# A complex power table on VectorE: rows of 80 bytes, second products in a tile of their own, exponents in another order, and a new order of all steps

## The chip, the cores and the metric

The kernel runs on one core of a Trainium2 chip. A core has five engines that run side by side and meet through semaphores: TensorE (PE in the profile; its weight loads are PEld), VectorE (DVE), ScalarE (ACT), GpSimd (POOL) and SyncE (SP), which here issues the DMAs. The metric is the device time of one execution in microseconds (us); a time of the kernel is the median of several runs.

## The reference

Two branches on the same input `x` (2048 tokens x 512), mixed by a gate per token:

```python
g = sigmoid((x * gate_w).sum(-1, keepdims=True))
a = A(x)      # attention in 4 segments of 512 tokens, 32 heads of 16, with a running memory
b = B(x)      # state-space convolution over all 2048 tokens, per channel
return g * a + (1 - g) * b
```

Branch B builds a kernel of 2048 lags for each of the 512 channels from 128 complex states, and convolves by FFT:

```python
logdA = dt * (A_re + 1j * A_im)
l = arange(2048).astype(bf16)
P = exp(logdA[:, :, None] * l)                 # 512 x 128 x 2048 powers
K = einsum('dn,dnl,dn->dl', Cc, P, dt * Bc).real
y = irfft(rfft(pad(x)) * rfft(pad(K)))[:, :2048] + x * Dskip
```

Since `l` is rounded to bf16, only 640 different lags occur. Each is a sum of one of 20 exponents and one of 32 exponents, so the powers are products of two small tables.

## The kernel before

**Branch A.** For each of 4 segments and 4 groups of 8 heads, PE projects q, k and v and makes the scores in five parts (`scores`, tags A0, B0, C, A1, B1). ACT takes each part's exponential, 128x2048 at a time (L1128, 80 in all); DVE applies the causal mask to half of them (L1140). PE multiplies by v, DVE normalises (L1100 to L1103). The result goes through a DMA transpose or PE into the tile oT.

**Branch B, tables.** `ssm_powers` squares z = exp(dt A) nine times, so that `pws[(k, h)]` holds z to the power 2^k for half h of the channels. `tables(c)` runs four times, once for each 128 channels. It fills two tables in SBUF, with 4 bytes (two states in bf16) for each entry:
- table F has 20 slots, one for each exponent of `F_EXP`, and 4 spare slots behind them: a row of 24 slots is 96 bytes, and there are 128 rows, 64 in each of two planes (real and imaginary);
- table G has 32 slots, for multiples of 8, and 8 spare ones: rows of 160 bytes.

Four slots of F and one of G are copied in (L1253, L1256; engine chosen by the order). The others come from `cmul` (L1226): it multiplies n slots at `src`, `src + sstep`, ... by z^(2^k) and writes them to the n slots from `dst`. A complex product is two real products and a sum. With sources that are neighbours (`sstep == 1`), one DVE instruction makes both products (L1236), the second going to the spare slots `sp`. Otherwise there are two instructions, one for each product (L1241). Then a sum (L1245) adds the spare slots, planes exchanged, to the destination. F has six such steps, G also six. Then 128 small matmuls a table (`64x40`, tags lag) multiply G by F, and the lag values go through `kex` and four DMAs to the tile KTT.

**Branch B, convolution.** `conv` has 32 steps u. A spectrum of x comes from `x_level1` through DRAM (Zx) and a matmul (X). The constants CD come by DMA into one of 4 buffers. PE makes the spectrum of K from CD and KTT, a cast takes it to SBUF, DVE multiplies (L1371, tags Y), PE transforms back (tags V), a cast takes V to SBUF, and a DMA puts its rows into the tile V2. Steps 0 to 15 fill V2[0], steps 16 to 31 fill V2[1].

**The end.** `finals` makes 16 results of 128x512. Each is a sum in PSUM of matmuls over oT and `wo` (tags fin, fih) and over V2 (fir reads V2[0], fis V2[1]). Results 0 to 7 are taken out in two parts and pass a float32 tile (L1405 prepares it, L1427 adds, L1441 writes out), results 8 to 15 in one scaled copy (L232 on ACT or L233 on DVE).

**The order.** Nothing is scheduled while the kernel is built. The string `ORDER` lists every operation by its number, in the order in which each engine runs it; `a` or `v` behind a number says whether a copy that either engine could make runs on ACT or DVE (`evac`: L229 and L232 on ACT, L230 and L233 on DVE), and the numbers behind a slash choose the buffers. `replay` reads it and `emit` puts the semaphore waits in. DMAs are operations of SP in the same list, issued in their order: one that waits holds up those behind it.

Of the kernel before, what the change touches and what calls it, by code (L numbers as in the profile page):

```python
# [8 lines left out]
BF16 = mybir.dt.bfloat16  # L9
# [365 lines left out]
15/0 16/0 9/0 37/4/0 38 0/0 10/1 31/0/0 32a 7/0 47/0 13/2 1203/0 29/5 30a 17/1 40/1 18 19 39/2 46/3 42/4 20 49/5 43 44  # L375
45 21 48/6 50 41/7 53/0 65/1 55/8 51 52 1214/6/0 5/0 66/2 12/3 54/9 58/0 68/7 56/10 1209/3/1 60/11 1/0 57 72/1 59/12
63/0 61/13 73v/0 62 11/4 3/0 70/0 71 64 1215v 69v/0 82/1 83/2 84 27/0 202/0 33/0/1 34a 218/0 203 67v 23/0 4/0 96/3
26/0 14/5 94/2 95 85v/1 76/3 1211/1 206/0 1212a 1216/0 213/2/0/0 209/4 106/0 77/4 214a 86 1210a 263/1/1/1 264a 97v/2
204 35/2/2 268/5/0/0 189/5 210/0 108/6 36a 74 24/0 223/3 22/0 107 118/1 78 390/0 109v/3 120/7 215 184/0 227/1/1/1
820/0 1213 119 88/2 89/1 224a 269 270 605/0 187/3 98 130/0 1217a 110 131/2 1206/2/1 133a/4 132 185/1 121a/5 122  # L380
407/3/1 228 1204/0 216/6/0 217a 134 144/3 253/0/0 254 111 408a 142/2 1224/1 2/0 230 123 1205a 255 90 190/0 1207a 186/0
188 192/1 1019a/0 145v/6 143 219/3 75 220v 606/0 146 157v/7 232/0/1 1023 271 233 154/3 155/7 1024 135 607 821/2 100/2
229 234 99 1027 1218 822 156 1028 158 221/3 1029 1018v/0 211/0 1030 1221/0/0 205/0 222a 1219/1 1017a 147 1220a 1208
1245/0 265 159 168/6 1031 241/0/2 242 212/0 1222a 243 1032 306/2/2/2 307a 1015a 225/3 226a 236/0/3 237 1223 235/1 238
266/0/1 308 1230/2/1 267a 1231a 1038 87 1016a 239 240 169v/8 279/0/1 166/3 167 28/0 1020 102/0 1225/3/0 1226a 1227/0
244 245/1 1228a 1232/2 280 1229 281 1237/3/0 1021 1039 350/0/2 351a 249/0/3 250 246 1022 170 1233a 1234 231/0/0 272
247/0 347/2/3/0 251 248/1 284/0/2 1238a 285 1040 178v/9 348a 391/3 392 171 273/0 252 286 1263/2/1 1264a 256 1025
1235/3 1236a 257 258/2 393 275/0/3 276 277 1026 1261/0 179 180 1041 311/2/1/1 312 352/3/0/0 259 1239 353 1033 101
112/3 260 1034 313 1035 296/0/0 297 298 354 309/1/0 314 278/2 1262a 1242/3/0 310a 1265 292/0/3 293 355 1036 113/5 282
283 315/0 1037 1243a 1042 356 291/1 114 1043 294 124/2 349 287 1240/3 1241a 1044 1045 288/3 1046 357 333/0/1 334 335  # L390
1051/3/0 1052 395/1 1053 126/2 125 136/3 1055/0 1056 1057a 193 191 1054a 207 320/0/2 137/3 138 321 1047/0 322 289 1048
1049 1050a 1061/0 150/7 295 208 1066v/0 299 300 1064v/0 1063v 1248/3/1 1070 1062v 301/4 1065a 1067 1071 302 1266/1
316/0/3 317 1249a 318 1068 290/1 1246/0 1247a 1060 1059 396/3/0/1 397a 1069 148/2 1074 337/0/0 338 319/2 323 139v/3
1072 149 1073 303 1080 409/0 339 1075 140 1076 410a 160/1 1077 325/0/3 103a/0 104 324 1244 1250 326 505/3/1/2 141 1081
327 1078 398 1082 457/1/1 458a 506a 359/0/2 360 361 332/0 336 91a/1 340 328 161/6 341 342/5 1083 115v/5 304 1084 105
1253/1/0 1254a 1251/3 1252a 1255 329/0 343 1089 363/0/1 364 330 1269/1/1 79v/2 365 399/3/0 1079 127a/8 400a 1090
368/0/3 369 1270a 116 370 117 1272/3/0 411/1 92 412a 80 1273a 162 81 93 172/0 331/1 376/0/0 377 362/2 366 367 371
405/1 1091 378 163v/4 406a 1274/3 344 128 1058 345 413/0/1/1 129 414 380/0/2 1085 175v/6 1275a 1086 1092 381 382 375/1
379 261 415 1267/3 1268a 164 454/0/2/0 455a 165 418/0/1 419 420 1271 1087 176 177 1093 456 383 1088 384 385/1 624/3/0
461/0 625a 462/0/0/0 463 174/2 403/1 464 422/0/3 423 465 1098/3/0 372/2 424 1099 386 1276 1094/0 1095 1096 1097a 404  # L400
1100 1101a 435/0/0 416 387/1 373 151v/9 374 173 181v/7 1291/0 436 437 1102/1 1103 1277/0/1 274 1258/2/0 1259a 1256/3
439/0/2 1257a 1112v/0 1278a 440 1322/1 1113v/0 441 1111a 152 557/2/2 1104v 1106 558a 153 1117 182 421/1 1279/3 1118
507 1260 388 1121 427/0/1 428 1284/0/0 1110v 1122 1109v 1280a 425 1105 426 183 1282/2 1123 1114 429 1285a 1124 262/0
417/3/1 466 478/0/3 1283a 479 434/0 1115 1281 1125 1116 438 442 1126 6/0 1119 608 480 430 1107 431/3 1120 1309/2 443
444/4 1127 626/2 432 467 1128 401/0 627a 1286 1108 473/0/0 474 475 8/0 305 445 669/2/3/1 459/1 402 469/0/1 433/0 470
670a 1129 513/3/1/1 471 1301/0 194/1 446 508/2/0 509a 1132 1130 195/0 486/0/2 487 514 515 488 1310/0/0 1131 460 472/2
476 1287/0 1302/1/0 1303a 1288/1 1289/3/1 477 1290a 1311a 1136 1133 1137 1134 481 490/0/1 1138 491 492 485/1 489 1135
554/3/0/0 555a 1314/2 1292/0/1 1139 1140 1304/3 1293a 346 535/0/0 536 537 556 614/3/1 1370/4 615a 1305/0/2 1306a 394/0
493 494 495/0 1307/4 610/0 824 496 482/5 562/5/0/0 1294/6 563 565 1145/3/0 564 358 1141/0 1308a 1146 1295a 1147 1148a
1340/1 483 484/1 516 1142 1143 1144a 539/0/3 540 497 541 498/1/1/0 1317/2 1149/0 1150 1151a 1327/0 199/0 196 671 512/0  # L410
# [98 lines left out]
F_EXP = [1, 3, 6, 8, 2, 4, 262, 264, 258, 260, 5, 7, 520, 516, 776, 772, 1032, 1288, 1544, 1800]  # L509
# [1023 lines left out]
```

## Time and profile before

| | us |
|---|---|
| median of 3 runs | 300.8 (299.62 to 302.68) |
| the profiled execution, its own time | 297.4 |
| its span, first to last instruction | 295.6 |
| PE busy | 256.1 |
| DVE busy, 609 instructions | 270.6 |
| ACT busy, 326 instructions | 262.1 |
| mean granted TensorE clock | 0.971 |

The profile is of one execution. A row of its groups has the line, the engine, the operation, what is written and read with shapes, the number of instructions, their busy time together, the mean length of one in ns, and the idle time of the engine just before them with what ended it. An instruction's length reaches from its start to its result; on DVE and ACT the next one can start a little before that. The line of a copy is that of the helper `evac`.

### The profile page before, as it was taken

What the parts mean: (1) busy time and instruction counts of PE and PEld (TensorE: products, weight loads), DVE (VectorE), ACT (ScalarE), POOL (GpSimd) and SP (SyncE); (2) the same over time, 40 slices, a digit from 0 to 9 for tenths busy, and PEclk for the clock granted to TensorE, in tenths of its full rate; (3) what the DMA queues carried; (4) which work ended last, traced back from release to release, by engine and by line L of the source; (5) the groups of instructions that cost most, each with busy time, mean ns of one, the idle gap of its engine ahead of it and who ended that gap; (6) DMA issues with size and microseconds to landing.
All of it is one profiled execution on the core that took longest, in us unless ns stands there. A gap on an engine that the chain in (4) does not pass through costs nothing.

```text
span 295.6 us, 8579 instructions
## 1 busy us (share of the span) xinstructions
PE 256.1 (87%) x3517; PEld 151.7 (51%) x3563; DVE 270.6 (92%) x609; ACT 262.1 (89%) x326; POOL 3.2 (1%) x9
## 2 busy tenths in 40 slices
PE   5786887789878797899998899999998999999992
PEld 2343344464445563576663655555554454547661
DVE  2989999989999999999999999999899999987792
ACT  5989999989999999999999999999999999985120
POOL 2000000000000000000000000000000000000000
PEclk9979799957999999999999999999999999999999
DMA  5999712105224358226754368767676867994124
GB/s 127 259 259 202 219 39 86 42 2 159 55 54 124 115 157 202 84 65 164 178 104 118 81 190 233 199 178 200 185 220 162 221 196 177 243 215 120 38 109 174
DMA packets 60600, 44.00 MB, mean 149 GB/s; under 512 B 34577, under 2 KB 55954, under 8 KB 60562
## 3 DMA queue, kind: packets, MB, share of 16 engines
q1 hardware_dynamic: 60562, 43.46, 55.7%
q8 instruction: 28, 0.46, 0.7%
q14 instruction: 10, 0.08, 0.1%
HBM read 22.08 MB, written 7.86 MB: 101 GB/s over the span
## 4 chain that ended last, share of the span: by engine, by line
DVE 48%; PE 26%; ACT 18%; issue 5%; DMA 1%; SPq 0%; DVEq 0%
PE psum L704 25%; DVE sb L1236 13%; ACT sb L1128 10%; DVE sb L1245 9%; ACT sb L229 6%; DVE sb L1241 4%; DVE sb L230 3%; DVE sb L1103 1%; DVE sb L1140 1%; DVE sb L850 1%; DVE sb L849 1%; DVE sb L1182 1%; DVE sb L1009 1%; DVE sb L1371 1%; DVE sb L857 1%
## 5 line engine op out<-in xcount | busy, mean ns | idle before, releaser
L704 PE MATMUL psum<-sb 128*128 128x17 bf16 (+13 forms) x3429 | 250.9, 238 | 32.8 <-ACT sb L1128 12.9
L704 PEld LDWEIGHTS psum<-sb 128*128 128x128 bf16 (+5 forms) x3475 | 145.6, 101 | 133.2 <-ACT sb L1128 33.6
L1128 ACT ACTIVATE sb<-psum 128x2048 bf16<-128x2048 f32 x80 | 151.6, 1895 | 4.6 <-PE psum L704 3.8
L229 ACT ACTIVATE sb<-psum 128x512 bf16<-128x512 f32 (+4 forms) x162 | 88.3, 595 | 10.4 <-PE psum L704 8.3
L1236 DVE TENSOR_TENSOR sb<-sb 128x1024 bf16<-128x1024 bf16 (+3 forms) x36 | 48.8, 1358 | 0.1
L230 DVE CAST sb<-psum 128x512 bf16<-128x512 f32 (+3 forms) x51 | 31.0, 619 | 3.1 <-PE psum L704 2.9
L1245 DVE TENSOR_TENSOR sb<-sb 128x512 bf16<-128x512 bf16 (+3 forms) x48 | 33.4, 700 | 0.1
L1140 DVE TENSOR_TENSOR sb<-sb 128x1024 bf16<-128x1024 bf16 (+1 forms) x40 | 22.7, 579 | 1.1 <-ACT sb L1128 0.9
L1371 DVE TENSOR_TENSOR sb<-sb 128x1024 bf16<-128x1024 bf16 x32 | 21.8, 681 | 0.9 <-ACT sb L229 0.4
L1241 DVE TENSOR_TENSOR sb<-sb 128x512 bf16<-128x512 bf16 (+1 forms) x24 | 15.2, 632 | 0.5 <-ACT sb L229 0.3
L1103 DVE TENSOR_TENSOR sb<-psum,sb 128x256 bf16<-128x256 f32 x32 | 13.5, 421 | 0.4
L232 ACT ACTIVATE sb<-psum,sb 128x512 bf16<-128x512 f32 x5 | 3.4, 687 | 11.5 <-PE psum L704 11.5
L848 ACT ACTIVATE sb<-sb 128x512 f32<-128x512 f32 x18 | 11.4, 656 | 0.3 <-DVE sb L849 0.3
L1427 DVE SCALAR_TENSOR_TENSOR sb<-psum,sb 128x512 f32<-128x512 f32 x8 | 5.9, 748 | 2.9 <-PE psum L704 2.9
L1182 DVE TENSOR_TENSOR sb<-psum,sb 128x512 bf16<-128x512 f32 x12 | 8.3, 689 | 0.3
L849 DVE TENSOR_TENSOR sb<-sb 128x256 f32<-128x256 f32 x18 | 7.6, 420 | 1.1 <-ACT sb L848 1.0
L1100 DVE RECIPROCAL sb<-psum 128x16 f32<-128x16 f32 x32 | 8.0, 251 | 0.4 <-PE psum L704 0.3
L1059 ACT ACTIVATE sb<-sb 128x512 bf16<-128x512 bf16 x12 | 7.6, 633 | 0.1
L850 DVE SCALAR_TENSOR_TENSOR sb<-sb 128x256 f32<-128x256 f32 x18 | 7.6, 420 | 0.0
L1008 ACT ACTIVATE sb<-psum 128x512 bf16<-128x512 bf16 x12 | 7.3, 623 | 0.0
L857 DVE CAST sb<-sb 128x512 bf16<-128x512 f32 x15 | 6.3, 423 | 0.0
L1441 DVE SCALAR_TENSOR_TENSOR sb<-psum,sb 128x512 bf16<-128x512 f32 x8 | 5.6, 744 | 0.4 <-PE psum L704 0.3
(75 smaller groups left out, 112.4 us busy)
## 6 DMA issues: line engine op xcount, KB each, us to landing
sb<-sb SPq DMA_DIRECT2D x64, 128.0 KB, 3.6
sb<-c_DN SPq DMA_DIRECT2D x32, 224.0 KB, 3.1
scr_Z<-sb SPq DMA_DIRECT2D x16, 256.0 KB, 2.3
sb<-scr_Z SPq DMA_DIRECT2D x16, 256.0 KB, 3.7
sb<-in_A_x_dram SPq DMA_DIRECT2D x5, 512.0 KB, 4.9
sb<-c_DN SPq DMA_DIRECT2D x16, 160.0 KB, 2.9
out_dram<-sb SPq DMA_DIRECT2D x8, 256.0 KB, 2.1
scr_O<-sb SPq DMA_DIRECT2D x12, 128.0 KB, 2.8
```

The costliest lines, as they stand in the source:

```text
L229: fa = lambda e: e.activation(dst(), src(), ACT.Copy)
L230: fd = lambda e: e.tensor_copy(dst(), src())
L704: mm = lambda e, o_, l, r_, st, sp, **kw: e.matmul(o_, lhsT=l, rhs=r_, start=st, stop=sp, skip_group_check=True, **kw)
L848: op("ACT", ("As", 512), lambda e, sq=sq, Z=Z: e.activation(ap(sq, n=512), ap(Z, n=512), ACT.Square), r=[Z], w=[sq], key=PW[h] + PWS * k)
L1103: op("DVE", ("V1", 256), lambda e: e.tensor_tensor(ap(o1, gi * 16, [[128, 4], [32, 4], [1, 16]]), ap(T, dims=[[68, 4], [17, 4], [1, 16]]), ...
L1128: o = op("ACT", ("Ax", 2048), lambda e, P=P, pT=pT: e.activation(ap(pT, n=2048), ap(P, n=2048), ACT.Exp, scale=0.25), r=[P], w=[pT])
L1140: op("DVE", ("V2", 128 * nb), lambda e, pT=pT, dims=dims: e.tensor_tensor(ap(pT, dims=dims + [[1, 128]]), ap(pT, dims=dims + [[1, 128]]), ...
L1182: op("DVE", ("V1", 512), lambda e: e.tensor_tensor(ap(o2, 0, [[128, 4], [16, 8], [1, 16]]), ap(P2, 0, [[256, 4], [17, 8], [1, 16]]), ap(R2 ...
L1236: op("DVE", ("V2n1" if n == 1 else "V2", 512 * n), lambda e: e.tensor_tensor(ap(tile, 2 * dst, [[2 * (sp - dst), 2], [2 * ne, 128], [1, 2 ...
L1241: op("DVE", ("V2", 256 * n), lambda e, half=half: e.tensor_tensor(ap(tile, 2 * (sp if half else dst), [[2 * ne, 128], [2, n], [1, 2]]), ap ...
L1245: op("DVE", ("V2n1" if n == 1 else "V2", 256 * n), lambda e: e.tensor_tensor(D_(), D_(), ap(tile, 2 * sp + ne * 128, [[-ne * 128, 2], [2 * ...
L1371: op("DVE", ("V2", 1024), lambda e, Y=Y, XAB=XAB, K3=K3, Ke=Ke, xo=xo: e.tensor_tensor(ap(Y, dims=[[512, 2], [1, 512]]), ap(XAB, xo, [[512 ...
```

## The change

The spare slots of F go away, so that its rows are 80 bytes long, and the second product of a step of F is written to a new tile `t2` of its own, densely. The two tiles have the size of the old one together. Every step of F is now three instructions (two products and a sum); G's steps stay as they were. The exponents stand in another order in F's slots, and the six steps and the four copied slots are changed to fit it: sources that lay 5 apart (slots 0 and 5) are now neighbours (5 and 6), one step has sources 4 apart (slots 1 and 5), the others 1 or 2. `F_EXP` also decides where a lag stands in the constant CD, whose size stays. The cost names `"V2"` and `"V2x"` are for the planner outside the kernel and have no effect here. `ORDER` is another list throughout: it holds 12 more operations, all on DVE, and 76 of the free copies change engine, 40 from ACT to DVE and 36 from DVE to ACT; the buffers and the places of the DMAs differ too.

```diff
-F_EXP = [1, 3, 6, 8, 2, 4, 262, 264, 258, 260, 5, 7, 520, 516, 776, 772, 1032, 1288, 1544, 1800]
+F_EXP = [1, 5, 3, 7, 6, 4, 2, 8, 262, 260, 258, 264, 516, 520, 772, 776, 1032, 1288, 1544, 1800]
...
-    FP = mkpool("F", 12288, 1)
+    FP = mkpool("F", 10240, 1)
+    t2P = mkpool("t2", 2048, 1)
...
-        EF, EG = NF + 4, NG + 8
+        EF, EG = NF, NG + 8
...
-            spp = parts(dct, tile, sp, 1)
-            if sstep == 1:
+            D_ = lambda: ap(tile, 2 * dst, [[ne * 128, 2], [2 * ne, 64], [1, 2 * n]])
+            if sp:
+                spp = parts(dct, tile, sp, 1)
                 op("DVE", ("V2n1" if n == 1 else "V2", 512 * n), lambda e: e.tensor_tensor(
                     ap(tile, 2 * dst, [[2 * (sp - dst), 2], [2 * ne, 128], [1, 2 * n]]), ap(tile, 2 * src, [[0, 2], [2 * ne, 128], [1, 2 * n]]),
                     ap(pw, cl * 512, [[2, 256], [0, n], [1, 2]]), ALU.mult), r=rd + [pw], w=wr + spp + [tile])
-            else:
-                for half in range(2):
-                    op("DVE", ("V2", 256 * n), lambda e, half=half: e.tensor_tensor(
-                        ap(tile, 2 * (sp if half else dst), [[2 * ne, 128], [2, n], [1, 2]]), ap(tile, 2 * src, [[2 * ne, 128], [2 * sstep, n], [1, 2]]),
-                        ap(pw, cl * 512 + 256 * half, [[2, 128], [0, n], [1, 2]]), ALU.mult), r=rd + [pw], w=(spp if half else wr) + [tile])
-            D_ = lambda: ap(tile, 2 * dst, [[ne * 128, 2], [2 * ne, 64], [1, 2 * n]])
-            op("DVE", ("V2n1" if n == 1 else "V2", 256 * n), lambda e: e.tensor_tensor(
-                D_(), D_(), ap(tile, 2 * sp + ne * 128, [[-ne * 128, 2], [2 * ne, 64], [1, 2 * n]]), ALU.add), r=spp, w=wr)
-        fm = lambda *a_: cmul(F, fp, EF, NF, *a_)
+                op("DVE", ("V2n1" if n == 1 else "V2", 256 * n), lambda e: e.tensor_tensor(
+                    D_(), D_(), ap(tile, 2 * sp + ne * 128, [[-ne * 128, 2], [2 * ne, 64], [1, 2 * n]]), ALU.add), r=spp, w=wr)
+                return
+            t2 = Tile(t2P, BF16)
+            run = lambda T, E, e0, st: ap(T, 2 * e0, [[2 * E, 128], [2 * st, n], [1, 2]])
+            for half in range(2):
+                op("DVE", ("V2x" if sstep > 2 else "V2", 256 * n), lambda e, half=half: e.tensor_tensor(
+                    run(t2, n, 0, 1) if half else run(tile, ne, dst, 1), run(tile, ne, src, sstep),
+                    ap(pw, cl * 512 + 256 * half, [[2, 128], [0, n], [1, 2]]), ALU.mult), r=rd + [pw], w=[t2] if half else wr + [tile])
+            op("DVE", ("V2", 256 * n), lambda e: e.tensor_tensor(
+                D_(), D_(), ap(t2, n * 128, [[-n * 128, 2], [2 * n, 64], [1, 2 * n]]), ALU.add), r=[t2], w=wr)
+        fm = lambda *a_: cmul(F, fp, EF, 0, *a_)
...
-        for e_, k_ in ((0, 0), (4, 1), (5, 2), (3, 3)):
+        for e_, k_ in ((0, 0), (6, 1), (5, 2), (7, 3)):
...
-        fm(1, 0, 5, 2, 1)
+        fm(1, 5, 1, 2, 0)
         gm(1, 0, 1, 1, 3)
-        fm(10, 0, 1, 2, 2)
+        fm(3, 1, 4, 2, 1)
...
-        fm(6, 2, 1, 4, 8)
-        fm(12, 3, 2, 4, 9)
+        fm(8, 4, 1, 4, 8)
+        fm(12, 5, 2, 4, 9)
...
-        fm(16, 12, 2, 2, 9)
+        fm(16, 13, 2, 2, 9)
         fm(18, 16, 1, 2, 9)
```

The arguments of `fm` are the first destination slot, the first source slot, the step between sources, the number of slots and the exponent k of the power 2^k. `ORDER` is left out here.

More of the change, by code (lines that the diff above doesn't have):

```diff
@@ L460 @@
[L460 to L462 removed]
+218/0 15/0 16/0 37/4/0 9/0 0/0 10/1 38 31/0/0 32a 47/0 7/0 40/1 29/5 30a 39/2 41/3 17/1 18 19 11/2 46/4 3/0 4/0 42/5
+43 1215/0 1221/2/0 1226/3/1 1228/0 48/6 53/0 49/7 44 45 55/8 65/1 20 1/0 54/9 50 68/6 51 12/3 52 58/0 56/10 57 72/1
+33/7/1 60/11 1223/4 73v/0 59/12 63/0 61/13 70/0 71 1222a 1227a 62 85v/1 84/2 78/3 82/1 83 1229a 66/2 97v/2 67v/0 76/2
@@ new lines @@
+477 1322/3/1 1400/4 433/0 446 1323a 1140 1141 1301/2/0 1302a 619 1314/0/1 1315a 1146 490/0/1 491 492 1142 481 2/0
+1306/3 1304/2/2 554/0/1/1 1305v 555a 1326/2 535/0/0 536 1147 1307a 485/0 537 1148/0 1329/3 1143 562/2/1/1 563 1379/0
+614/3/1 615a 346 489 493 1149 556 494 495/5 1319/4 1320a 482/0 1150/5/0 1151 1152 516 1153a 1334/0 823 358 483 565
+1154/3 1155 198 1156 484/1 1157a 564 539/0/2 824 540 460 496 402 825/0 1342/2 541 497 498/1/1/0 517/1 1158/0 1159
+1160a 499 500 1311 518/0/3 501 1169v/0 199 519 502 1173 512/0 1168v/0 1174 510/0 566 567 447/1/2/1 448 520 1178
@@ L463 @@
+1760a 1761
 """
```

168 lines of the change are left out of this document (80 added, 88 removed).

## The prediction

> **What bounds the kernel now.** I read the page first, then busy time by stretches, then the groups by shape, then the timeline of one table.
>
> ```profile
> DVE  2989999989999999999999999999899999987792
> ACT  5989999989999999999999999999999999985120
> ...
> DVE 48%; PE 26%; ACT 18%; issue 5%; DMA 1%; SPq 0%; DVEq 0%
> ```
>
> The digits are busy tenths in 40 slices of the span; the last row is the chain that ended last, by engine. DVE and ACT are full nearly throughout, and no single engine carries the chain. So the question is which of them is full in which stretch. The next view cuts the span at 30 us (after the preparation), at 165 us (after the last table), at 267 us (start of the last big exponential) and at 291.2 us (end of the last compute instruction). A row has the stretch, its length, the busy time (and instructions) of PE, weight loads, DVE, ACT and POOL, then the granted clock and the DMAs.
>
> ```profile
> 30.00:165.00 135.00, 115.20 (x1954) 71.84 (x1974) 132.21 (x284) 131.19 (x164) 1.32 (x2) 0.95 0.40 107
> 165.00:267.00 102.00, 96.52 (x1227) 54.27 (x1243) 95.89 (x226) 98.08 (x110) 0.00 (x0) 1.00 0.74 197
> 267.00:291.20 24.20, 23.15 (x185) 14.70 (x184) 18.98 (x33) 6.99 (x9) 0.00 (x0) 1.00 0.35 117
> ```
>
> From 30 to 165 us DVE and ACT are both at 97 to 98%: there a microsecond less on one of them alone buys little. From 165 to 267 us ACT leads (98.1 of 102). In the last 24.2 us PE is busy for 23.15, DVE for 19.0 and ACT for 7.0: there PE sets the end. All work on table F lies before 165 us, so a cheaper F is worth its price only where ACT gets lighter too.
>
> **The prices.** DVE groups by shape:
>
> ```profile
> L230 DVE CAST sb<-psum 128x512 bf16<-128x512 f32 x37 | 24.9, 686 | 3.1 <-PE psum L704 2.9
> ...
> L1236 DVE TENSOR_TENSOR sb<-sb 128x2048 bf16<-128x2048 bf16 x8 | 9.7, 1215 | 0.0
> L1245 DVE TENSOR_TENSOR sb<-sb 128x512 bf16<-128x512 bf16 x20 | 9.2, 459 | 0.1
> ...
> L1241 DVE TENSOR_TENSOR sb<-sb 128x512 bf16<-128x512 bf16 x16 | 8.7, 541 | 0.4 <-ACT sb L229 0.3
> ...
> L1140 DVE TENSOR_TENSOR sb<-sb 128x512 bf16<-128x512 bf16 x16 | 6.6, 419 | 0.5 <-ACT sb L1128 0.5
> L1241 DVE TENSOR_TENSOR sb<-sb 128x1024 bf16<-128x1024 bf16 x8 | 6.5, 814 | 0.0
> L857 DVE CAST sb<-sb 128x512 bf16<-128x512 f32 x15 | 6.3, 423 | 0.0
> L1405 DVE SCALAR_TENSOR_TENSOR sb<-sb 128x512 f32<-128x512 bf16 x8 | 6.0, 745 | 0.0
> ...
> L230 DVE CAST sb<-psum 128x256 bf16<-128x256 f32 x11 | 4.6, 415 | 0.0
> ```
>
> and single instructions of the first table, in order of time (start, length):
>
> ```profile
> 30.67 0.69 DVE L1236 TENSOR_TENSOR sb<-sb 128x1024 bf16<-128x1024 bf16 x1
> ...
> 33.27 0.33 DVE L230 COPY sb<-sb 128x256 bf16<-128x256 bf16 x1
> 33.41 0.69 DVE L1245 TENSOR_TENSOR sb<-sb 128x1024 bf16<-128x1024 bf16 x1
> ...
> 41.37 0.62 DVE L1241 TENSOR_TENSOR sb<-sb 128x512 bf16<-128x512 bf16 x1
> ...
> 56.45 0.48 DVE L1241 TENSOR_TENSOR sb<-sb 128x512 bf16<-128x512 bf16 x1
> ...
> 58.32 0.80 DVE L1236 TENSOR_TENSOR sb<-sb 128x1024 bf16<-128x1024 bf16 x1
> ```
>
> The copy at 33.27 is 0.33 long, yet its successor starts after 0.14. For ordinary tensor products the same overlap is about 0.085 us (an estimate from start-to-start times in this timeline), so every instruction is worth its length less 0.085.
>
> Dense products take 0.42 (128x512, L1140); G's sum of 128x1024, at 33.41, takes 0.69, and I use 0.68 for that shape. F is dearer. One half of the step to slots 1 and 2, whose sources lie in slots 0 and 5, takes 0.62 (row at 41.37); the half from slots 12 and 14, two apart, 0.48 (56.45). The joint product of slots 18 and 19 takes 0.80 where G's same shape takes 0.69 (58.32 against 30.67). The halves of the step to 12..15, sources 3, 5, 7, 9, take 0.814.
>
> **Part 1, the six F steps of a table.** Before, 15 instructions: four halves of 512 (mean 0.541, 2.16), two of 1024 (1.63), two joint products at 0.80 (1.60), one joint at 1.215, four small sums at 0.46 (1.84), two sums at 0.68 (1.36): 9.81, less 15 x 0.085 gives 8.53 us. After, every step is two halves and a sum, 18 instructions. I price each from the nearest row:
> - Slots 1, 2 from adjacent 5, 6: halves between 0.42 and 0.62. I take 0.47, the close-source row, with a sum of 0.46: 1.40.
> - Slots 3, 4 from 1 and 5, four apart: between 0.48 and 0.62. I take 0.62, as five apart is nearest: 1.70.
> - Slots 8..11 from 4..7: dense runs of four; the joint instruction at 1.215 shows no surcharge, so 0.68 three times: 2.04.
> - Slots 12..15 from 5, 7, 9, 11: between 0.68 and 0.81. I take 0.70: in groups of four slots the old sources fell into three groups, the new ones into two, and the pair that shared a group (12, 14) was near the dense price: 2.08.
> - Slots 16, 17 from 13, 15: 0.48 twice and 0.46: 1.42.
> - Slots 18, 19 from 16, 17: half of 0.80 + 0.085 is 0.44, twice, and 0.46: 1.34.
>
> Sum 9.98, less 18 x 0.085 is 8.45: 0.08 us less per table, 0.3 us over four. With every half and small sum at its dense price a table comes to 9.24 - 1.53 = 7.71, 3.3 us less in all. If 80-byte rows made every run of two cost 0.62 (sums 0.48) and every half of 1024 0.82, it would be 11.52 - 1.53 = 9.99, or 5.8 us more. The three extra instructions thus eat what the closer sources give.
>
> The Trainium skill has a rule for my choice at 12..15: SBUF — State Buffer, Specifications (TRN2), gives 16-byte cachelines that want at least two hits each; four slots are 16 bytes here, and the trace's 0.62, 0.48 and 0.814 agree with it. The Trainium skill also has a rule that speaks against the change: its page Vector Engine (DVE) Microarchitecture Reference, section 5.2 Measured stream behaviour on trn2, gives full rate only for runs of two adjacent words that start on an 8-byte boundary, 1.30 instead of 1.054 ns per column for pairs on an odd word. Slots 1, 2 and 5, 6 are such odd pairs, and 12..15 would keep 0.81: an estimate by that page is some 1 us more over four tables than mine (a table's two halves at 12..15 0.11 dearer each, the two at 1, 2 0.01). The trace's 0.48 for two hopping sources speaks against it, and so does the 0.80 of an even, adjacent pair in 96-byte rows.
>
> The new tile's reuse adds one wait: the second half of a step must stand behind the previous step's sum. Both are on DVE, in order, and the first half lies between them, so nothing waits that is not already behind. The matmuls that read F read 40 dense elements as before; I cost the new row length at zero there, with PE's 20 idle us between 30 and 165 us as cover.
>
> **Part 2, work moved between DVE and ACT.** The order also chooses the engine of each copy. Counting the two lists, DVE takes five more 512-wide casts from PSUM (0.60 each after overlap), two more scaled ones (0.66, as L1405), eight more small table copies (0.14), and gives up six 256-wide casts (0.33), two 320-wide (0.40, between the 256 and the 512) and three L857 casts (0.34): 3.0 + 1.3 + 1.1 - 2.0 - 0.8 - 1.0 = +1.6 us. The ACT rows are:
>
> ```profile
> L229 ACT ACTIVATE sb<-psum 128x512 bf16<-128x512 f32 x128 | 74.3, 625 | 8.0 <-PE psum L704 7.6
> ...
> L229 ACT ACTIVATE sb<-psum 128x256 bf16<-128x256 f32 x21 | 7.9, 395 | 0.1
> ...
> L229 ACT ACTIVATE sb<-sb 128x256 bf16<-128x256 bf16 x9 | 4.9, 563 | 0.0
> ...
> L232 ACT ACTIVATE sb<-psum,sb 128x512 bf16<-128x512 f32 x5 | 3.4, 687 | 11.5 <-PE psum L704 11.5
> L856 ACT ACTIVATE sb<-sb 128x512 bf16<-128x512 f32 x5 | 3.2, 658 | 0.0
> ```
>
> ACT's successors start 0.1 early (0.2 after the small copies): 5 x 0.52 + 2 x 0.59 + 8 x 0.36 given up, 6 x 0.30 + 2 x 0.33 + 3 x 0.56 taken: -2.5 us.
>
> **Part 3, where it lands.** I cut both lists at the last of the 80 big exponentials. Behind it DVE has 35 instructions instead of 32: two scaled results, two products of L1405 and one cast more, two products less, +2.3 us. So ahead of it DVE has 1.6 - 2.3 - 0.3 = -1.0 us. ACT has three casts behind it as before and two scaled results fewer (1.2), so -1.3 ahead. With both nearly full there, the last exponential comes 1.0 to 1.3 us earlier. Behind it PE has 65 steps instead of 66, DVE 19.0 + 2.3 = 21.3 of 24.2: hidden by PE. SP's order is new too, and a load stands behind whatever is queued before it. For the loads of CD, the conv's constants, the list keeps at least 8 PE steps between the one that frees a buffer and the one that needs its next content, against 9 before: I cost it at nothing. Sum: -1.1 us. The profiled execution took 297.4 us (span 295.6), the median of the runs is 300.8, a factor 1.0114: 296.3 profiled, 299.7 us as a median.
>
> **The rivals.**
> - Faster: F falls to its dense prices (-3.3) and the moved work counts too: DVE -0.7 - 3.3 = -4.0 ahead of the last exponential. For it: the old surcharges are plain (0.80 against 0.69, 0.814 against 0.68). Against it: ACT falls by 1.3 only; the rest must come out of ACT's 7.7 us of gaps between 30 and 267 us. 297.4 - 4.0 = 293.4, median 296.7. Chance 0.25.
> - Slower by the rows: the short hop of 80 bytes makes pairs as dear as far sources, +5.8 - 0.7 = +5.1 on DVE between 30 and 165 us, where it has 2.8 us to spare at most. 302.5, median 306.0; it decides from some 0.9 us per table on. Against it: four-slot runs were at the dense price at 96 bytes. Chance 0.10.
> - Slower in the tail: the last spectrum product to finish is now V26, whose copy stands on DVE behind six normalisation instructions and two L1427; its rows must land before any result's last matmul.
>
> ```profile
> sb<-sb SPq DMA_DIRECT2D x64, 128.0 KB, 3.6
> ```
>
> Uncovered, a 0.69 cast and that landing are 4.3 us in which PE waits, 297.4 - 1.1 + 4.3 = 300.6, median 304.0. Against it: 12 of PE's 65 steps stand between V26 and the first of those matmuls, some 12/65 x 23.15 = 4.3 us of cover, just enough (before, it was 16 steps behind the last such product, V29). It decides once DVE reaches V26's copy over 1 us after PE has its product. Chance 0.14.
> - The new order is a reshuffle and nothing else: the forecast, with zero instead of -1.1, 300.8. It belongs to the forecast's case.
>
> **How the numbers follow.** The forecast's own case (296.3 profiled, give or take the 2 us of its choices) has 0.51. A measurement of this kernel can tell about 1%, as its three runs span 299.6 to 302.7. Faster by over 1%: 0.25. Slower by over 1%: 0.10 + 0.14 = 0.24. Within: 0.51. The range runs from 295.8, a little below the faster rival, to 303.8, just short of the tail rival, and leaves out the row rival.
>
> **What would show it.** F's lines: halves of 512 at 0.42 to 0.48 except those of slots 3, 4 near 0.62; halves of 1024 near 0.70. DVE busy near 272, ACT near 259. In the stretch after the last big exponential PE still over 95% busy, with no wait above 1 us for a spectrum DMA. It is wrong if a half of 1024 costs 0.8 again, if the first result's wait in the tail exceeds some 5 us, or if the last exponential does not come earlier.

## The result and the profile after

| | before | after |
|---|---|---|
| median | 298.27 us (295.11 to 302.68, 18 runs) | 294.37 us (291.44 to 298.56, 18 runs) |
| ratio after to before | | 0.9877 [0.9848, 0.9907] |
| profiled execution | 297.4 us | 296.62 us |
| forecast, as a ratio (299.7 to 300.8) | | 0.9963 |

The changed kernel is 1.2% faster, three times the forecast, and its median lies 1.4 us below the forecast range. Part of that distance is the base: the three runs from which the forecast was scaled had a median of 300.8 us, the eighteen of the comparison 298.27. On the base of the forecast the measured ratio gives 300.8 x 0.9877 = 297.1 us. What has to be explained is the ratio: -1.2% for -0.4%. Here and below a ratio is formed from those runs of each kernel that lie within 1.5% of its fastest, so it is not exactly the quotient of the medians.

The profiled execution of the changed kernel was 2.3 us above its own median, so its stretches are not compared with those of before to less than that. Two other profiles of the changed kernel, e3 and e18 below, are of executions nearer to their medians and are used where the total counts. The page of this one, with span, busy time by engine and the chain that ended last:

```profile
span 294.8 us, 8578 instructions
PE 253.0 (86%) x3518; PEld 150.6 (51%) x3563; DVE 269.5 (91%) x625; ACT 258.9 (88%) x322; POOL 3.2 (1%) x9
...
PE 35%; DVE 24%; ACT 23%; DMA 11%; issue 4%; SPq 2%; DVEq 0%
```

ACT has 3.2 us less work (262.1 before), DVE 1.1 less although it took copies over. Busy time by the stretches of the prediction (PE, weight loads, DVE, ACT, POOL, granted clock, DMA):

```profile
30.00:165.00 135.00, 112.39 (x1951) 69.92 (x1964) 129.59 (x297) 130.43 (x165) 1.32 (x2) 0.96 0.42 111
165.00:267.00 102.00, 95.92 (x1243) 56.03 (x1259) 95.27 (x224) 97.98 (x107) 0.00 (x0) 1.00 0.73 198
267.00:291.20 24.20, 22.48 (x163) 14.01 (x164) 20.72 (x35) 4.24 (x7) 0.00 (x0) 1.00 0.32 114
```

While tables are made (30 to 165 us) DVE and ACT are 5.4 and 4.6 us from full, against 2.8 and 3.8 before: this execution waited more. Still the last big exponential began earlier, at 265.62 us instead of 266.89. From the timeline (start, length):

```profile
265.62 1.88 ACT L1130 ACTIVATE sb<-psum 128x2048 bf16<-128x2048 f32 x1
```

In e3 and e18 it began still earlier, at 261.51 and 262.99 us. Behind it come 29.2 us to the end of the span in all three, 28.7 before: the tail grew by 0.5 us.

The F steps by shape (products L1248, sums L1251):

```profile
L1248 DVE TENSOR_TENSOR sb<-sb 128x512 bf16<-128x512 bf16 x32 | 14.1, 458 | 0.0
...
L1248 DVE TENSOR_TENSOR sb<-sb 128x1024 bf16<-128x1024 bf16 x16 | 10.6, 682 | 0.0
...
L1251 DVE TENSOR_TENSOR sb<-sb 128x512 bf16<-128x512 bf16 x16 | 7.4, 464 | 0.0
...
L1251 DVE TENSOR_TENSOR sb<-sb 128x1024 bf16<-128x1024 bf16 x8 | 5.5, 687 | 0.1
```

and single ones of the first table:

```profile
33.45 0.42 DVE L1251 TENSOR_TENSOR sb<-sb 128x512 bf16<-128x512 bf16 x1
...
40.53 0.60 DVE L1248 TENSOR_TENSOR sb<-sb 128x512 bf16<-128x512 bf16 x1
...
42.31 0.61 DVE L1251 TENSOR_TENSOR sb<-sb 128x512 bf16<-128x512 bf16 x1
...
49.08 0.68 DVE L1248 TENSOR_TENSOR sb<-sb 128x1024 bf16<-128x1024 bf16 x1
...
55.86 0.42 DVE L1248 TENSOR_TENSOR sb<-sb 128x512 bf16<-128x512 bf16 x1
```

Every pair is at the dense 0.42 but one: slots 3 and 4 take 0.60, in the products (40.53) and in the sum (42.31). All fours are at 0.68. A table takes 8 x 0.458 + 4 x 0.682 + 4 x 0.464 + 2 x 0.687 = 9.62 us by lengths, less 18 overlaps of 0.085 it is 8.09, against 8.53 before: 0.44 us per table, 1.8 us in all, where the forecast had 0.3.

### The profile page after: what moved, and what is told of

It is laid out like the page before. It is cut to its first block, busy times and chain, and to the rows that moved or that the text cites. A ratio compares the mean times of both kernels' runs of the same rounds, so it can differ in the third digit from the quotient of the medians.

```text
span 294.8 us, 8578 instructions
## 1 busy us (share of the span) xinstructions
PE 253.0 (86%) x3518; PEld 150.6 (51%) x3563; DVE 269.5 (91%) x625; ACT 258.9 (88%) x322; POOL 3.2 (1%) x9
## 4 chain that ended last, share of the span: by engine, by line
PE 35%; DVE 24%; ACT 23%; DMA 11%; issue 4%; SPq 2%; DVEq 0%
PE psum L706 34%; ACT sb L1130 15%; ACT sb L229 6%; DVE sb L1239 4%; DMA sb<-sb 4%; DVE sb L230 3%; DVE sb L1248 2%; DMA sb<-scr_Z 2%; SPq L225 2%; DMA sb<-in_A_x_dram 2%; DMA sb<-c_DN 1%; DVE sb L1251 1%; DVE sb L1242 1%; DVE sb L1377 1%; DVE sb L1184 1%
## 5 line engine op out<-in xcount | busy, mean ns | idle before, releaser
L706 PE MATMUL psum<-sb 128*128 128x17 bf16 (+13 forms) x3430 | 248.4, 237 | 35.0 <-ACT sb L1130 15.0
L229 ACT ACTIVATE sb<-psum 128x512 bf16<-128x512 f32 (+5 forms) x165 | 88.5, 591 | 8.4 <-PE psum L706 5.8
L1239 DVE TENSOR_TENSOR sb<-sb 128x4096 bf16<-128x4096 bf16 (+3 forms) x24 | 37.5, 1565 | 1.3 <-DMA sb<-sb 1.3
L230 DVE CAST sb<-psum 128x512 bf16<-128x512 f32 (+2 forms) x48 | 30.8, 655 | 3.2 <-PE psum L706 2.4
L1248 DVE TENSOR_TENSOR sb<-sb 128x512 bf16<-128x512 bf16 (+1 forms) x48 | 24.6, 533 | 0.0
L1242 DVE TENSOR_TENSOR sb<-sb 128x2048 bf16<-128x2048 bf16 (+3 forms) x24 | 20.4, 851 | 0.0
L232 ACT ACTIVATE sb<-psum,sb 128x512 bf16<-128x512 f32 x3 | 2.1, 687 | 17.1 <-PE psum L706 17.1
L1251 DVE TENSOR_TENSOR sb<-sb 128x512 bf16<-128x512 bf16 (+1 forms) x24 | 12.9, 538 | 0.1
L1103 DVE TENSOR_TENSOR sb<-sb 128x16 f32<-128x16 f32 x32 | 5.6, 175 | 0.4
```

Source lines behind the costliest of these rows:

```text
L229: fa = lambda e: e.activation(dst(), src(), ACT.Copy)
L230: fd = lambda e: e.tensor_copy(dst(), src())
L706: mm = lambda e, o_, l, r_, st, sp, **kw: e.matmul(o_, lhsT=l, rhs=r_, start=st, stop=sp, skip_group_check=True, **kw)
L1239: op("DVE", ("V2n1" if n == 1 else "V2", 512 * n), lambda e: e.tensor_tensor(ap(tile, 2 * dst, [[2 * (sp - dst), 2], [2 * ne, 128], [1, 2 ...
L1242: op("DVE", ("V2n1" if n == 1 else "V2", 256 * n), lambda e: e.tensor_tensor(D_(), D_(), ap(tile, 2 * sp + ne * 128, [[-ne * 128, 2], [2 * ...
L1248: op("DVE", ("V2x" if sstep > 2 else "V2", 256 * n), lambda e, half=half: e.tensor_tensor(run(t2, n, 0, 1) if half else run(tile, ne, dst, ...
```

## The experiments

Two things were open: what makes F's steps cheap, and which part of the 1.2% comes from F, which from the order and from the engines of the copies. Each ratio below is against runs of the kernel before on the same chip. Runs e1 to e4 were made on one chip, e5 to e12 on a second, e13 to e15 on a third, e16 to e18 on a fourth.

**e1: the new F alone.** Shapes, exponents and `t2` of the changed kernel, but the order and the engines of the kernel before, its numbers moved up by the 12 operations that are new (one line of `ORDER` as it then stands):

```diff
...
+1292a 425 1111 426 183 1294/2 1130 1120 429 1297a 1131 262/0 417/3/1 466 478/0/3 1295a 479 434/0 1121/0 1293 1132 1122
...
```

> Table F as changed (80-byte rows, own tile for the second products, new exponents), but every other step in the order and on the engines of the kernel before. If the gain is F's alone, this is as fast as the changed kernel, a ratio to before near 0.988. If it is the order's alone, the ratio is 0.997 to 1.000. By my sum of the changed profile's lengths F saves 0.43 us of DVE a table, 1.7 us in all, so with nothing hidden the ratio is 0.994, and with half of it hidden behind ACT 0.997. F's halves of 512 keep 0.415 us except those with sources four apart (0.60).

Measured: 1.0004 [0.9976, 1.0032]. DVE's busy time fell by 1.8 us, as it should, and the time did not move:

```profile
PE 258.3 (88%) x3563; PEld 150.2 (51%) x3563; DVE 268.8 (91%) x621; ACT 261.4 (89%) x326; POOL 3.2 (1%) x9
```

**e2: the new order alone.** The changed order and its engines, with F as before:

```diff
-F_EXP = [1, 5, 3, 7, 6, 4, 2, 8, 262, 260, 258, 264, 516, 520, 772, 776, 1032, 1288, 1544, 1800]
+F_EXP = [1, 3, 6, 8, 2, 4, 262, 264, 258, 260, 5, 7, 520, 516, 776, 772, 1032, 1288, 1544, 1800]
...
-        EF, EG = NF, NG + 8
+        EF, EG = NF + 4, NG + 8
...
```

> The old table F (96-byte rows, spare slots, old exponents, joint products) in the new order of all other steps. If the order alone gives the gain, a ratio near 0.988; if F alone, 1.000; if both add, 0.994. Lengths of F's steps as in the kernel before (0.62, 0.80, 0.814).

Measured: 0.9938 [0.9907, 0.9968]. Its page:

```profile
PE 256.2 (87%) x3563; PEld 150.3 (51%) x3563; DVE 271.8 (93%) x613; ACT 258.3 (88%) x322; POOL 3.2 (1%) x9
```

ACT lost 3.8 us against the kernel before, DVE gained 1.2. So the order is worth 0.6% without the new F.

**e3: the changed kernel beside them.** No edit.

> The changed kernel once more, beside the others: ratio 0.985 to 0.991 and a profile of an execution nearer to its median.

Measured: 0.9898 [0.9853, 0.9944]. Taken together with e2, the new F gives 0.9898 / 0.9938 = 0.996 in the new order; alone (e1) it gave nothing. By the medians of these ratios the two parts do not add up on this chip; but their product, 1.0004 x 0.9938 = 0.994, lies inside the interval of e3, so that this is not shown.

**e4: rows of 96 bytes.** The changed kernel with four unused slots behind each row of F:

```diff
-    FP = mkpool("F", 10240, 1)
+    FP = mkpool("F", 12288, 1)
...
-        EF, EG = NF, NG + 8
+        EF, EG = NF + 4, NG + 8
...
```

What is left out makes the room: two small tiles (`grA`, `grS`) lie elsewhere.

> The changed kernel with F's rows at 96 bytes again (four unused slots behind the 20), everything else as changed; two small tiles lie elsewhere to make room. If the row length made pairs dear, the pair halves and sums of the steps to 16, 17 and 18, 19 go back from 0.415 to 0.47 us and the kernel loses some 0.8 us (four tables, four halves and two sums at 0.05, less the overlap), a ratio near 0.990. If only the 16-byte groups of slots matter, all lengths stay and so does the time, ratio 0.988.

Measured: 0.9851 [0.9806, 0.9897], no loss that can be told (its six runs spread from 291.7 to 297.6 us, and the loss that was expected is 0.8), but the steps did change (products L1246, sums L1249 here):

```profile
PE 255.7 (87%) x3563; PEld 149.6 (51%) x3563; DVE 271.1 (92%) x625; ACT 258.5 (88%) x322; POOL 3.2 (1%) x9
...
L1246 DVE TENSOR_TENSOR sb<-sb 128x512 bf16<-128x512 bf16 x32 | 15.4, 499 | 0.0
...
L1246 DVE TENSOR_TENSOR sb<-sb 128x1024 bf16<-128x1024 bf16 x16 | 10.5, 677 | 0.0
...
L1249 DVE TENSOR_TENSOR sb<-sb 128x512 bf16<-128x512 bf16 x16 | 8.1, 508 | 0.0
```

The steps on pairs are 0.04 us dearer in the mean (0.499 for 0.458, 0.508 for 0.464), the fours are not (0.677 for 0.682). DVE's busy time is 1.9 us above e3's 269.2; with the old F (e2) it was 2.6 above. So the shorter row makes most of what the new F saves, net of its 12 extra instructions.

**e5: the new order with the old engines.** Every copy that may stand on either engine back on the engine it had before (40 and 36 of them). One line of `ORDER`:

```diff
-1018v/0 222a 230 1225 1023 1231/0 232/0/1 156/4 233 821/3 822 1024 87 223/2 224v 5/0 234 75 605/0 1028 146 1029
+1018v/0 222a 230 1225 1023 1231/0 232/0/1 156/4 233 821/3 822 1024 87 223/2 224a 5/0 234 75 605/0 1028 146 1029
```

> The changed kernel, table F and order as they are there, but every copy that may stand on either engine back on the engine it had before. Theory 1, ScalarE ahead of the last big exponential sets the end and the gain comes from the copies that the change moves from it to VectorE: ScalarE's busy sum goes from 258.4 back to about 261 to 262 us, VectorE's from 269.2 to about 268, the ratio to the kernel before is 0.996 to 1.000. Theory 2, the order of the steps gives the gain by itself, whichever engine does the copies: the ratio stays at 0.985 to 0.992.

Measured: 1.0754 [1.0663, 1.0845]. Neither theory had this. The busy time is that of the kernel before, and the rest is waiting. Its page, and what ACT waited for over the whole span (total, times, longest):

```profile
PE 261.7 (82%) x3563; PEld 149.9 (47%) x3563; DVE 269.9 (85%) x621; ACT 262.5 (82%) x326; POOL 3.5 (1%) x9
...
ACT sb L229 <- PE psum L706: 18.8, 23, 2.8
ACT sb L232 <- PE psum L706: 12.1, 3, 5.9
ACT sb L1130 <- PE psum L706: 11.3, 17, 2.9
```

The three rows come to 42.2 us; in the kernel before the same three were 8.3, 11.5 and 3.8. My reading is that an order is made for its engines: a copy put back into ACT's list at the place that it had in DVE's holds up all that stands behind it. No single copy was followed to show it. This run doesn't separate engines from order; it shows that they can't be exchanged one by one.

**e6 and e7: ten table copies alone.** In the old order, nine of the small table copies moved from ACT to DVE and one back, as the change has them; e6 with the new F, e7 with the old one. One of the edits:

```diff
-188 192/1 1019a/0 145v/6 143 219/3 75 220v 606/0 146 157v/7 232/0/1 1023 271 233 154/3 155/7 1024 135 607 821/2 100/2
+188 192/1 1019v/0 145v/6 143 219/3 75 220v 606/0 146 157v/7 232/0/1 1023 271 233 154/3 155/7 1024 135 607 821/2 100/2
```

> The kernel before with the new table F in the old order (as in the first run of this study, ratio 1.000), and in it alone the engines of ten table copies as the change has them: nine from ScalarE to VectorE, one the other way. ScalarE loses about 2.9 us, VectorE gains about 1.1 and stays 0.6 below the kernel before. Theory 1 (ScalarE sets the end): ratio about 0.992 (0.989 to 0.995). Theory 2 (the order gives it): ratio about 1.000 (0.997 to 1.003).

> The kernel before with its old table F and its old order, and in it alone the engines of the same ten table copies changed. ScalarE loses about 2.9 us, VectorE gains about 1.1. Theory 1: faster, but by less than with the new F, ratio about 0.994 to 0.997, for VectorE has no room made by F. Theory 2: ratio about 1.000 to 1.004.

Measured: 1.0004 [0.9956, 1.0051] and 1.0068 [1.0027, 1.0110]. ACT's busy time fell by 2.4 us (e6: 259.7; 1.7 against e1) and 1.9 us, without effect. DVE's rose by nearly as much, 1.4 us (e6 against e1) and 1.8 us (e7), where 1.1 had been expected. The theory that ACT's sum alone sets the end fell here; e7 is even 0.7% slower. In the profiled executions ACT waits longer for PE ahead of the tail (up to 260 us: 10.1 us in e6 and 11.7 in e7, 5.9 before).

**e8: what makes a step cheap.** The kernel before, in its order, with rows of 80 bytes and `t2`, but the exponents in their old order (its steps are then `fm(1, 0, 5, 2, 1)` and `fm(12, 3, 2, 4, 9)` again). Only its profile was taken.

> The kernel before in its old order, with rows of 80 bytes and the second products in a tile of their own, but with the exponents in their old order. Only the lengths of F's steps are asked for. If the 16-byte groups of the sources set the length: the halves from slots 3, 5, 7, 9 take 0.82 us, those from slots 0 and 5 about 0.60, the pairs 16,17 and 18,19 about 0.415. If the tile of its own or the shorter rows did it: the four halves 0.68, all pairs about 0.415.

From the timeline of its first table:

```profile
43.65 0.59 DVE L1248 TENSOR_TENSOR sb<-sb 128x512 bf16<-128x512 bf16 x1
...
55.88 0.84 DVE L1248 TENSOR_TENSOR sb<-sb 128x1024 bf16<-128x1024 bf16 x1
...
57.38 0.84 DVE L1248 TENSOR_TENSOR sb<-sb 128x1024 bf16<-128x1024 bf16 x1
...
59.18 0.43 DVE L1248 TENSOR_TENSOR sb<-sb 128x512 bf16<-128x512 bf16 x1
```

Sources 0 and 5 take 0.59 (0.59 to 0.60 in seven of eight, 0.50 in one), sources 3, 5, 7, 9 take 0.84, and the pair 16, 17 takes 0.43: what the groups of four slots (16 bytes) said. So the new exponents, not the tile of its own, make the step to 12..15 cheap (0.68 in the changed kernel). In all they are worth little: DVE is busy for 269.4 us here and for 268.8 in e1, for with the new exponents one pair still costs 0.60 in its products (slots 3 and 4) and now 0.61 in its sum too.

**e9 to e12: the spectrum loads cut loose.** In e1's profile TensorE waits at 115 us for two loads, a constant (M0) and the first spectrum rows, which are read back from DRAM just after they were written, and then runs at half its clock. Here the loads Zx read the constant M instead (same bytes), so that they wait for no write; the convolution's half of the output is thereby left out. e9 is e1 with this edit, e10 the kernel before, e11 is e6, e12 the changed kernel.

```diff
-                S.dma(lambda Zx=Zx: ap(Zx, n=1024), lambda pi=pi, t=t: bass.AP(Zd, pi * 1048576 + t * 512, [[8192, 128], [1, 1024]]),
-                      262144, r=[dZ], w=[Zx], key=kx - 5)
+                S.dma(lambda Zx=Zx: ap(Zx, n=1024), lambda t=t: hM[:, (t // 2 % 4) * 1024:(t // 2 % 4) * 1024 + 1024],
+                      262144, w=[Zx], key=kx - 5)
```

> The first run's kernel (new F in the old order), in which the loads of the sixteen spectrum inputs Zx read as many bytes of the constant M in place of the rows that the kernel has just written, so that no load waits for a write; the spectrum half of the output is left out by it, all instructions and transfers stay. Theory A, round trip: with the cheaper F, TensorE reaches the first two spectrum steps (115 us) before M0 and Zx0 have landed, waits 1.2 us there, its granted clock halves for 3.4 us, and F's saving is lost by it; without the wait the saving comes out: 1 to 2 us less than the kernel before with the same edit, ratio to the unedited kernel before 0.992 to 0.996, no half clock between 110 and 130 us. Theory B, ScalarE's unchanged list sets the time in the old order whatever the loads do: ratio 0.999 to 1.002.

> The kernel before with the same edit of the Zx loads (they read the constant M, wait for no write; that half of the output is left out). Both theories: the round trip is hidden behind VectorE's F steps here, so 0.998 to 1.001. If it falls to 0.995 or below, the round trip cost the kernel before as well and the edit measures something else than F.

> New F, old order, ten table copies on the engines of the changed kernel, and the same edit of the Zx loads. Theory A: the 1.7 us PE gap at 114.6 us and the 7 us of half clock behind it go; F's saving and ScalarE's 2.6 us both come out, ratio 0.988 to 0.993. Theory B': the old order's other waits take it, 0.998 to 1.002.

> The changed kernel with the same edit of the Zx loads. Theory A: the new order has the round trip covered (no wait of TensorE for these loads, no half clock between 100 and 290 us in its profiles), so it stays at the changed kernel's ratio, 0.985 to 0.990. If it falls below 0.983, the round trip costs there too.

Measured: 0.9967 [0.9926, 1.0009], 1.0039 [1.0002, 1.0076], 1.0020 [0.9981, 1.0059] and 0.9927 [0.9894, 0.9960]. The edit costs 0.4% by itself (e10; the interval begins at 0.02%). Like against like, the new F gives 0.9967 / 1.0039 = 0.993, the whole change 0.9927 / 1.0039 = 0.989, and F with the table copies 0.998. That spoke for the theory that this wait eats F's saving, though the intervals of e9 and e10 overlap a little.

**e13 to e15: the round trip begun earlier.** The round trip is the write of the spectrum rows to DRAM and their load back. Three operations of the old order moved, with nothing left out: the two casts of the last rows of the spectrum (xl1.15) ahead of the exponential in front of them, and their write (1298) straight behind the one before (1293); 429 is the exponential. e13 is e1 with it, e14 the kernel before, e15 is e6.

```diff
-1292a 425 1111 426 183 1294/2 1130 1120 429 1297a 1131 262/0 417/3/1 466 478/0/3 1295a 479 434/0 1121/0 1293 1132 1122
...
-1298 1114 473/0/0 474 475 8/0 305 445 669/2/3/1 459/1 402 469/0/1 433/0 470 670a 1137 513/3/1/1 471 1313/0 194/1 446
+1292a 425 1111 426 183 1294/2 1297a 1295a 1130 1120 429 1131 262/0 417/3/1 466 478/0/3 479 434/0 1121/0 1293 1298 1132 1122
...
+1114 473/0/0 474 475 8/0 305 445 669/2/3/1 459/1 402 469/0/1 433/0 470 670a 1137 513/3/1/1 471 1313/0 194/1 446
```

> The first run's kernel (new F, old order) with three steps of the order moved and nothing left out: the two casts of the last spectrum rows (xl1.15) on ScalarE ahead of the big exponential that stood before them, and the write of these rows on the DMA queue straight behind that of xl1.14. The write then starts about 2 us earlier and M0 and Zx0 land about 1 us earlier, near 114.5 to 115 us. Theory A, round trip and the half clock behind it: TensorE's wait for these loads falls below 0.5 us, the clock stays whole between 110 and 130 us, ratio 0.992 to 0.997. Theory B, ScalarE's unchanged sum of work sets the time in the old order: 0.999 to 1.002.

> The kernel before with the same three moves. Both theories: the round trip is covered there already, so 0.998 to 1.002.

> New F, old order, ten table copies on the engines of the changed kernel, and the same three moves. If the wait at the spectrum loads was all that held back ScalarE's relief, 0.988 to 0.993. If the old order has other waits for it, as the run with the cut loads says (1.002), 0.997 to 1.002.

Measured: 0.9893 [0.9861, 0.9925], 0.9989 [0.9957, 1.0020] and 0.9954 [0.9917, 0.9991]. By e13 the new F with three moved operations would have brought as much as the whole change.

**e16 to e18: the same on one chip.** e1, e13 and the changed kernel once more, side by side.

> New F in the old order once more, now on one chip beside the kernel with the three moves, for the two were measured on different chips. Theory A, the exposed round trip: 0.997 to 1.003 again, 0.6 to 1.2% above the kernel with the moves. If it comes out at 0.993 or below, the difference between the two was one of the chips and F's saving was never hidden.

> New F, old order and the three moved steps once more. Theory A: 0.987 to 0.993 again.

> The changed kernel beside them: 0.985 to 0.991. If the order searched anew holds more than the cover of the round trip, it is 0.3% or more below the kernel with the three moves; if the cover is its whole part beside F, the two agree within 0.3%.

Measured: 0.9951 [0.9918, 0.9984], 0.9989 [0.9953, 1.0026] and 0.9922 [0.9884, 0.9960]. The theory fell: on the same chip the kernel with the three moves is no faster than the one without. The moves did what they were made for. In e1 TensorE waited for both loads (waits of TensorE from 113 to 120 us), and the clock fell behind the wait (stretches of 2 us; the third number from the end is the clock):

```profile
PE psum L706 <- DMA sb<-c_M: 0.7, 1, 0.7
PE psum L706 <- DMA sb<-scr_Z: 0.4, 1, 0.4
...
116.00:118.00 2.00, 1.62 (x25) 1.08 (x26) 2.00 (x5) 1.46 (x3) 0.00 (x0) 0.82 1.27 223
118.00:120.00 2.00, 2.00 (x29) 1.18 (x28) 2.00 (x1) 1.61 (x1) 0.00 (x0) 0.50 0.54 198
120.00:122.00 2.00, 2.00 (x16) 1.03 (x15) 2.00 (x5) 1.25 (x3) 0.00 (x0) 0.82 0.00 0
```

In e17 no such load is waited for in that window:

```profile
PE psum L704 <- ACT sb L1128: 0.7, 1, 0.7
```

But in e16, the same kernel as e1, the wait is there again and the clock stays whole:

```profile
PE psum L706 <- DMA sb<-scr_Z: 0.6, 1, 0.6
PE psum L706 <- DMA sb<-c_M: 0.3, 1, 0.3
...
116.00:118.00 2.00, 2.00 (x49) 1.48 (x46) 2.00 (x3) 1.70 (x3) 0.00 (x0) 1.00 0.92 274
118.00:120.00 2.00, 2.00 (x18) 1.11 (x17) 2.00 (x3) 1.95 (x4) 0.00 (x0) 1.00 0.12 39
```

The half clock was an event of that execution, not a property of the kernel: between 114 and 126 us it also stands in the profiles of e2, e6, e7 and e11, with the old F (e2, e7) as with the new one. And the wait alone is worth less than can be measured.

## Why the prediction was wrong

**The direction was right, the size was not.** What the forecast called the faster rival is what came in numbers: it stood at 296.7 / 300.8 = 0.986, the measured ratio is 0.988. Its chance had been put at 0.25. That it came so near is in part luck: it took all of 3.3 us from F, of which 1.8 to 2.6 came, and the moved copies and ACT gave more than it had taken.

**The first step that failed: the price of F's pairs.** The prediction took its pair prices (0.47, 0.48, 0.46 for sums) from rows of the 96-byte table and read them as the price of sources that lie close but hop. They were the price of the long row: e4 shows the same steps at about 0.04 to 0.05 more with 96 bytes than with 80. The sum had no term for the row's length, and the rival that had one gave it the wrong sign (short rows dearer, +5.8 us). Its price for the fours was right (0.68, and 0.70 taken for 0.68 at 12..15), its price for the products of slots 3, 4 nearly (0.62 taken, 0.60 measured), and the sum there was taken too low (0.46, measured 0.61). The other three pair steps are all 0.42 instead of 0.44 to 0.48, 0.1 to 0.2 us less each. Of the gain 0.3 us was forecast, 1.8 measured on DVE in the old order (e1) and 2.6 in the new one (e2 against e3). The all-dense sum of the faster rival has a slip: by the prediction's own prices it is 12 x 0.42 + 6 x 0.68 = 9.12, not 9.24.

**The second step that failed: the work that falls away ahead of the last big exponential.** The prediction counted 1.0 us less on DVE and 1.3 less on ACT there, and so an exponential that starts 1.0 to 1.3 us earlier. Cut at the start of that exponential, the profiles of the kernel before and of the changed one in e3 and e18 give (stretch, length, PE, weight loads, DVE, ACT, POOL, clock, DMAs):

```profile
0.00:266.89 266.89, 232.81 (x3335) 136.85 (x3379) 251.49 (x577) 255.00 (x318) 3.19 (x9) 0.97 0.59 153
...
0.00:261.51 261.51, 233.89 (x3375) 135.76 (x3376) 247.11 (x589) 252.81 (x316) 3.21 (x9) 0.97 0.60 156
...
0.00:262.99 262.99, 230.24 (x3375) 134.56 (x3376) 247.10 (x589) 252.01 (x315) 3.21 (x9) 0.99 0.59 155
```

DVE has 4.4 us less, ACT 2.2 and 3.0 less, and the exponential starts 5.4 and 3.9 us earlier. Of DVE's 4.4 the order makes 1.7 (e2 has 249.75), F the other 2.6. DVE's figure is the same to 0.1 us in e10 and e14; ACT's moves by 0.7 us between those runs of the old list (254.4 to 255.1), so its part is known less well.

**The two rules.** The rule of 16-byte lines (the Trainium skill, SBUF — State Buffer, Specifications (TRN2)) agrees with the trace wherever it speaks: 12..15 at 0.68 with two slots in each line against 0.84 with 3, 5, 7, 9 (e8), 1 and 5 or 0 and 5 at 0.60, and slots 3, 4, which straddle two lines, dear even in the sum. It has nothing on the length of the row, which cost 0.05 a pair. The rule of even pairs (the Trainium skill, Vector Engine (DVE) Microarchitecture Reference, 5.2 Measured stream behaviour on trn2) does not hold for these products of bf16 pairs (the page measured streams of 32-bit words): slots 1, 2 and 5, 6 start on an odd word and run at 0.42, the dense price.

**"A cheaper F is worth its price only where ACT gets lighter too."** This was half right. New F in the old order, with ACT's work unchanged, gave 1.0004 and 0.9951, with the three moved operations 0.9893 and 0.9989, and 0.993 in the cut pair: 0.9953 in the mean, so some 1.4 of its 1.8 us came out (give or take 0.6, from the spread of the five); each single ratio could have been read as all or nothing. In the new order it gave 0.996. ACT relieved at DVE's cost gave nothing (e6, e7, e11; e15, with the three moves, 0.9954, no more than the new F alone), and the two busy times moved by nearly the same. The two engines hand work to each other through PE in fixed orders; that a saving on one comes out in part fits that, but no single saving was followed to the end. The forecast's own way of counting, half of what both lose ahead of the last big exponential, would have given (0.7 + 1.8 + 1.3) / 2 = 1.9 us with F at its price in e1, less 0.5 for the tail: 1.4 us or 0.5%. With the whole lists as measured it gives (4.4 + 2.2) / 2 = 3.3 in e3 and (4.4 + 3.0) / 2 = 3.7 in e18, less 0.5: 2.8 and 3.2 us. For the table copies in the old order, e6 and e7, it gives next to nothing, as measured. So the way of counting is not contradicted, and what it was given was too small.

**The moved copies.** By starts from one to the next, the copies of ACT that moved from ahead of the last big exponential come to some -1.3 us in e2, as forecast, but its whole list there has 2.3 us less (252.70). DVE lost 1.5 by starts for 0.7 forecast. The order alone is 0.6% (e2), 1.8 us; the forecast's count gives 1.0 less 0.5.

**The tail.** The forecast left it unchanged; it is 0.5 us longer. That holds in the profiles of the new order (29.2 us, 30.5 in e5) against those of the old one (28.7 to 28.8). It is work of PE and no wait; from the start of the last exponential to the end, in e1 and in e18:

```profile
265.75:294.50 28.75, 23.49 (x190) 14.83 (x188) 19.08 (x33) 7.10 (x9) 0.00 (x0) 0.95 0.31 108
...
262.99:292.20 29.21, 24.03 (x193) 15.13 (x191) 22.11 (x37) 5.62 (x7) 0.00 (x0) 0.99 0.31 109
```

PE has three matmuls and 0.5 us more there, where the forecast counted one step less. The rival that PE would wait there for the rows of V26 did not come: PE is busy for 23.92 of the 24.2 us from 0.1 us behind that start in e3 and e18, over 95% as the prediction asked. The rival of dear 80-byte rows fell with e4.

**What stays open.** Measured were 2.3 to 3.7 us (0.9922, 0.9898 and 0.9877 in the three comparisons); the count with the whole lists gives 2.8 and 3.2, from single executions, and its halving is the forecast's rule and not shown. Why ACT's list is shorter by more than its moved copies is open. So is the part of the clock. The mean granted clock of TensorE was 0.978 in 131 runs of the kernel before (one of 382.9 us left out, whose clock was 0.564) and 0.986 in 35 of the changed one. Within the runs of each kernel 0.01 of clock goes with 1.19 us (give or take 0.09, from 322 runs of all kernels but e5), so the difference goes with 0.9 us. That is a correlation and not to be added to the count: why the clock is higher with the new order, and whether it is the cause or follows from waits, no run here tells. The table copies in the old order, too, were not followed to the single wait that ate them.

## What to carry to other kernels

Price an instruction from a row with the same pitch, not only the same pattern: here the length of a row that nobody reads to its end was worth 1.9 us of DVE (e4 against e3), the new order of the exponents 0.6 (e8 against e1). In a kernel whose engines run fixed lists and wait for each other, a saving on one engine may come out only in part, and a move of single operations between lists made for other engines can cost more than it saves (7.5% in e5). When less than one per cent is at stake, compare on one chip and do it twice: the same kernel gave 0.9893 [0.9861, 0.9925] on one chip and 0.9989 [0.9953, 1.0026] on another, and a wait seen in one profile had seemed to explain it.

## What the runs showed of the hardware

- Products of pairs of 4-byte entries in rows of 80 bytes, 128x512: 0.42 us with both entries in one group of 16 bytes, whether the pair starts on an even or an odd entry; 0.60 with one in each of two groups, for sources as for the destination. Fours, 128x1024: 0.68 when each group that is touched gives two entries, 0.84 when two of three groups give one.
- Rows of 96 instead of 80 bytes add 0.05 us to a dense pair and nothing to a four (e4). Only these two lengths were run; what about the longer row costs the time, no run tells.
- TensorE's clock fell to half for about 3.4 us (0.82, 0.50 and 0.82 over 2 us each, an estimate that takes every loss as a halving) behind 1.1 us of waits for loads in e1 and stayed whole behind 0.9 us at the same place in e16. The Trainium skill (TensorE: Matmul & The Clock Gate, Why this matters for your kernels) warns of idle gaps of over some 3 us; here no single wait of TensorE between 113 and 120 us was longer than 0.7 us.
- The interval of a ratio holds for its chip and its runs: measured again on another chip, one kernel came out 0.5% lower (e1, e16), another 1.0% higher (e13, e17).
